# One fused kernel on one Trainium2 core: input sums of the gated layer by transfers instead of elementwise instructions, the expert table's zeros written in the attention stage, and four changes in the order of work

## The chip, the cores and the metric

The kernel runs on one core of one Trainium2 chip. The metric is the device time of one execution, in microseconds; the time of a kernel is the median of its runs.

The core's engines are TensorE (PE in the profile, with PEld its weight loads), VectorE (DVE), ScalarE (ACT), GpSimd (POOL) and SyncE (SP, which here issues transfers). Each works through its own queue of instructions in order. Transfers are issued by SP, ACT or POOL and carried by 16 DMA engines. Tiles live in SBUF, TensorE's results in PSUM banks.

## The reference

Attention over 4 batches, 8 heads, 576 positions and 64 channels, with two kinds of mask; then a gated layer, and then a routed layer with eight experts, of which each token takes one, or none:

```
scores = q @ k.T / 8                  # masked: heads 0-3 see the 32 last positions,
attn   = softmax(scores) @ v          # heads 4-7 every 32nd position before them
x      = attn as (2304 tokens, 512)
x      = (sigmoid(x @ w_gate) * (x @ w_val)) @ w_out         # 512 -> 1536 -> 512
run    = x @ w_skip > 0
e      = argmax(x @ w_gate8)          # over 8 experts, with softmax probability g
out    = x + g * (relu(x @ w1[e]) @ w2[e])   if run, else x  # 512 -> 1024 -> 512
```

## The kernel before

All products of the gated layer and of the experts are made in fp32 precision from two parts: a *high* part (a cast to fp32r on ACT) and a *low* part (the rest, x − high, usually on DVE). A product is three matmuls, high by high, low by high and high by low; the lines L593 to L595 are these three, whatever the product.

**Attention** (to about 131 us) runs in steps t = 0 to 34. What a step does, and in which order it is written, is a string of letters: `eSfEmIFnaNDTMRpDAaL`. `n` and `N` are the scaling of the softmax rows on POOL (`norm`, L314), `f` and `F` the transposes of the result on PE (`flip`, L323), `A` the product with the values (`apply_v`, L339), which copies its result from PSUM on DVE into the tokens' tiles `xf` (L351). `D`, `a` and `p` take one job from the queues of DVE, ACT and POOL. `L` (`step_loads`) fills these queues.

**The gated layer** saves products as Strassen's and Winograd's schemes do: a 2 x 2 block of operands is multiplied with seven products in place of eight. The tokens' operands of a *pair* of token units are the blocks B11, B12, B21 and B22, read from `xf`, and four sums: T1 = B12 − B11, T2 = B22 − T1, T3 = B22 − B12, T4 = B21 − T2 (`combine`, L417). There are three pairs (0, 1, 2) with two units each. `operand` queues the high and the low part of a block or sum. The weights' side has sums too (S1 to S4, `stage_sums`). The **block stage** (about 132 to 397 us) goes over blocks (f, p): weight block f by pair p, 7.28 us each, in the order of the list `BL`; in each, seven products go to the banks A to D of PSUM, and a previous block's results are gated and stored (`store`, L651 to L670) to tables in DRAM, some of them by accumulating transfers that POOL issues (L644). Between the products `background` takes jobs from the three queues by rate, and `need` forces one at once. `split_w` queues the high parts (L534) and low parts (L537) of a weight block: first three quarters of the plain weights, then the four sums. `weights` and `out_weights` queue the conversion of the input weights and of the output weights (`wo`, index arithmetic at L460 and after), in tiles whose places come free as the loads and stores before them end.

**The unit stage** (about 397 to 551 us) makes the output product in 63 steps (`NSTEP`), 21 for each pair; each step is one of the seven products for one of three groups g of channels. It loads tokens' tiles from the tables (`xt`, split at L985 on ACT and L993 on DVE) and weights. Work beside the products hangs on the steps by `at(k, ...)`: the routing of a finished token unit is `turn_back` (three router products on PE at L1086 and L1087, a reduction on DVE at L1089 and a copy on ACT), `pick` (the choice of the expert), and `place` (the rank in the expert's table; then POOL scatters the rows to the table `xs` in DRAM by index). The units of the last pair are u4 and u5. In `init_xs` a tile `zero` is filled by POOL (L1191) and written thirteen times by SP to `xs`, in steps 9 to 15, since the rows that no token takes must be zero and carry a marker.

**The experts** (about 551 to 732 us) read the rows of an expert from `xs`, make the two products (`hidden`, `output_steps`), and scatter the result to the output by index. The first expert's tokens are loaded and cast by `prep` at the end of the unit stage.

Of the kernel before, what the change touches and what calls it, by code (L numbers as in the profile page):

```python
# [23 lines left out]
def kernel(  # L24
# [305 lines left out]
    xf = {}  # L330

    def apply_v(it, s, pT):
# [10 lines left out]
        if ty == 0:  # L343
            for u, o, x, n in spans(b, HS * s, HS * s + HS):
                nc.vector.tensor_copy(xf[u][0][:, hp, o:o + n], pv[:, x - HS * s:x - HS * s + n])
            return
        cl0, ncls = SGRP[s][0], m * n // TPC
        pc = pv.rearrange("p (c t) -> p c t", t=TPC)
        for u, o, x, n in spans(b, 0, S):
            dst = xf[u][1][:, hp, o:o + n].rearrange("p (t c) -> p c t", c=STR)[:, cl0:cl0 + ncls, :]  # L350
            nc.vector.tensor_copy(dst, pc[:, :, x // STR:(x + n) // STR])  # L351
# [58 lines left out]

    def combine(p, nm, eng, parts, cost):

        e = nc.gpsimd if eng == "P" else nc.vector
        for part in parts:
            def fn(part=part):
                x, y = (source(p, z)[:, part, :] for z in SUMS[nm])
                e.tensor_tensor(source(p, nm)[:, part, :], x, y, op=ALU.subtract)  # L417
# [3 lines left out]
    def operand(p, nm, parts, hc, lc):  # L421

        for part in parts:
            def high(part=part):
# [4 lines left out]
                nc.scalar.copy(xh[p, nm][:, part, :], source(p, nm)[:, part, :])  # L429

            def low(part=part):
                h = xh[p, nm][:, part, :]
                nc.vector.tensor_tensor(
                    xl[p, nm][:, part, :], source(p, nm)[:, part, :], h.bitcast(F32), op=ALU.subtract)

            j = Job("A", hc, high, [sum_job[p, nm]] if nm[0] == "T" else [])
            x_jobs.setdefault((p, nm), []).append(Job("D", lc, low, [j]))
# [79 lines left out]
    def stage_sums(f):  # L517
        for i, x, y, op in ((4, 0, 1, ALU.add), (5, 4, 2, ALU.subtract), (6, 2, 0, ALU.subtract), (7, 3, 5, ALU.subtract)):
            def fn(i=i, x=x, y=y, op=op):
                nc.vector.tensor_tensor(stage(f, i), stage(f, x), stage(f, y), op=op)  # L520
# [152 lines left out]
    def period(k, prev):  # L673
# [24 lines left out]
        if prev:  # L698
            prev.mm("D", "A22", "T4", False)
            if prev.p == NP - 1:  # L700
                freed[prev.f].done = clock[0]
            prev.store("sC", "u4", 1)
# [115 lines left out]

    def step_loads(t):
        clock[0] += 1  # L820
        b, j = divmod(t, 8)
# [32 lines left out]
        if t == 22:  # L854
            combine(1, "T1", "P", HALVES, 1.0)
            operand(1, "B11", HALVES, 0.5, 0.5)
        if t == 26:
            for nm in ("T3", "T2", "T4"):
                combine(1, nm, "P", HALVES, 1.0)
            for nm in ("B21", "T3", "T2"):  # L860
                operand(1, nm, HALVES, 0.5, 0.5)
        if t == 30:
            combine(2, "T1", "P", HALVES, 1.0)
# [11 lines left out]
    for t in range(NS + 3):  # L875
        for c in ORDERS.get(t, "eSfEmIFnaNDTMRpDAaL"):
# [17 lines left out]
    raws_left += [(NC - 1, "o")]  # L894
# [12 lines left out]
    for nm in ("T3", "T2", "T4"):  # L907
        combine(2, nm, "D", WHOLE, 0.95)
    for nm in OPS:
# [90 lines left out]
    for f, p in BL:  # L1000
# [5 lines left out]
        if p == 0 and f > 1:  # L1006
            if f + 1 < NC:
                weights(f + 1, more_raw)
            for i in outs_of[f]:
# [63 lines left out]
    def turn_back(u, a):  # L1073
# [7 lines left out]
        for m in range(nb):  # L1081
# [6 lines left out]
            nc.scalar.copy(row[m][:, 256 * a:256 * a + 256].rearrange("p (c n) -> p c n", c=2), pr[:, :, 0:128])  # L1088
            nc.vector.tensor_reduce(  # L1089
                lp[:, m, a, :], pr[:, :, 128:NR].rearrange("p c (t n) -> p n c t", t=2), axis=AX.XY, op=ALU.add  # L1090
            )
            yield
# [94 lines left out]
    zero = []  # L1187

    def init_xs():
        zero = late.tile([128, TW], F32, tag="row", bufs=8, name="zero")  # L1190
        nc.gpsimd.memset(zero, 0.0)  # L1191
        nc.gpsimd.memset(zero[:, TW - 1:TW].bitcast(I32), 1 << 16)
        for i in range(NE * SLOTS // 128):
            nc.sync.dma_start(xs[128 * i:128 * i + 128, :], zero)
            if i % 2:
                yield

# [147 lines left out]
    gx = init_xs()  # L1345
    for k in range(9, 16):
        at(k, gx)
    for p in range(NP):
# [12 lines left out]
        if last:  # L1361
            for k, n in ((15, 1), (16, 2)):
                at(b + k, ta[1], n)
# [3 lines left out]
            for k in range(18, 21):  # L1367
                at(b + k, tb[1])
            g = later(lambda u=ua: place(u, rank_sums(rst[u][1])))
            for k in (19, 20):  # L1370
                at(b + k, g, 3)
# [438 lines left out]
```

## Time and profile before

| what | value |
|---|---|
| median of 3 runs | 747.71 us (747.09 to 747.77) |
| the profiled execution, whole | 746.98 us |
| its span in the trace | 745.3 us, granted TensorE clock 0.99 |
| PE busy | 706.2 us (95%), 4785 matmuls |
| PEld busy | 660.1 us (89%) |
| DVE busy | 561.6 us (75%) |
| ACT busy | 452.0 us (61%) |
| POOL busy | 258.9 us (35%) |
| moved by DMA | 158.57 MB, 213 GB/s in the mean |

The times of the table are of one profiled execution, except the first row. The span is the time from the first to the last instruction that the trace shows; the difference to the whole execution is work around it. A share is busy time over span. A row of a timeline has start, duration, engine, line of the kernel, operation, result and operands with their shapes, the count of equal instructions in a row, and in brackets how long the engine was idle before and which engine and tile ended that.

### The profile page before, as it was taken

The numbers are of one execution on the slowest core, as the hardware profiler recorded it, in microseconds if no ns is written. First come the engines' busy times: TensorE is split into PE (matmuls) and PEld (weight loads), VectorE is DVE, ScalarE is ACT, GpSimd is POOL, SyncE is SP. The second block draws the span as 40 slices with busy tenths as digits, with TensorE's granted clock in tenths as the row PEclk, the third lists the DMA queues.
The fourth block names the chain that finished last, engine by engine and source line by source line (L and its number), as shares of the span: only waits on it lengthen the run. The fifth ranks groups of instructions, "written<-read, shape, count | busy, mean of one in ns | idle before, by whom it ended". The sixth has DMA issues, their size and how long they took to land. (4 is left out here: it accounts for less than half of the span.)

```text
span 745.3 us, 14548 instructions
## 1 busy us (share of the span) xinstructions
PE 706.2 (95%) x4785; PEld 660.1 (89%) x4785; DVE 561.6 (75%) x1246; ACT 452.0 (61%) x1206; POOL 258.9 (35%) x289
## 2 busy tenths in 40 slices
PE   8999988999999999999998989999999999999992
PEld 5766666999999999999888989999988899999991
DVE  3799997989988888888876766677766666666650
ACT  5888986855555555555454855566644766676730
POOL 6577876021040211204033000402324644566611
PEclk9999999999999999999999999999999999999997
DMA  9999610296898888979599996879845687776710
GB/s 199 234 209 220 149 42 30 107 258 187 275 222 256 209 222 228 224 263 202 177 274 335 368 332 180 257 244 303 289 144 186 203 259 246 225 250 223 225 39 14
DMA packets 136857, 158.57 MB, mean 213 GB/s; under 512 B 60510, under 2 KB 105822, under 8 KB 136776
## 3 DMA queue, kind: packets, MB, share of 16 engines
q1 hardware_dynamic: 122072, 134.51, 58.6%
q0 software_dynamic: 11936, 19.66, 12.9%
q10 hardware_dynamic: 2768, 3.41, 1.3%
q8 instruction: 40, 0.66, 0.4%
q14 instruction: 41, 0.34, 0.1%
HBM read 103.49 MB, written 59.65 MB: 219 GB/s over the span
## 5 line engine op out<-in xcount | busy, mean ns | idle before, releaser
L644 POOL DMA_DIRECT2D gT<-sC x36 | 31.9, 1030 | 171.2 <-DVE sC L658 163.9
L301 ACT ACTIVATE sm<-psX,mx 96x128 f32<-96x128 f32 (+2 forms) x176 | 61.8, 375 | 10.1 <-DVE mx L295 7.9
L314 POOL TENSOR_TENSOR sm<-sm,rs 96x384 f32<-96x384 f32 (+2 forms) x64 | 55.5, 885 | 31.6 <-DVE rs L308 18.8
L985 ACT CAST xt<-xt 128x768 fp32r<-128x768 f32 (+1 forms) x74 | 53.9, 742 | 20.5 <-DMA xt<-gB 11.0
L993 DVE TENSOR_TENSOR xt<-xt 128x768 fp32r<-128x768 f32 (+1 forms) x74 | 60.6, 833 | 7.3 <-ACT xt L985 7.2
L639 DVE TENSOR_TENSOR u<-psD,u 128x384 f32<-128x384 f32 x70 | 38.7, 552 | 18.6 <-PE psD L595 18.3
L593 PE MATMUL psD<-xhT,wh 128*128 128x384 f32 x140 | 47.3, 338 | 1.6 <-DVE u L639 1.6
L595 PE MATMUL psA<-xhB,wl 128*128 128x384 f32 x140 | 47.0, 336 | 1.3 <-DVE wl L537 1.3
L595 PE MATMUL psD<-xhT,wl 128*128 128x384 f32 x140 | 47.1, 337 | 0.3 <-DVE wl L537 0.3
L594 PE MATMUL psD<-xlT,wh 128*128 128x384 f32 x140 | 47.0, 336 | 0.0
L594 PE MATMUL psA<-xlB,wh 128*128 128x384 f32 x140 | 46.8, 334 | 0.0
L593 PE MATMUL psA<-xhB,wh 128*128 128x384 f32 x140 | 46.8, 334 | 0.0
L595 PE MATMUL psB<-xhT,wl 128*128 128x384 f32 x140 | 46.8, 334 | 0.0
L593 PE MATMUL psB<-xhT,wh 128*128 128x384 f32 x140 | 46.8, 334 | 0.0
L594 PE MATMUL psB<-xlT,wh 128*128 128x384 f32 x140 | 46.8, 334 | 0.0
L632 ACT COPY psC<-psB 128x384 f32<-128x384 f32 x35 | 16.3, 465 | 43.4 <-PE psB L595 43.4
L1575 POOL DMA_INDIRECT out_dram<-xg x16 | 16.1, 1006 | 73.8 <-DVE xg L1574 65.4
L625 ACT COPY u<-psB 128x384 f32<-128x384 f32 x70 | 33.8, 483 | 11.3 <-PE psB L595 11.1
L1120 POOL COPY row<-lm_all 128x8 f32<-128x8 f32 x18 | 7.9, 478 | 90.1 <-DVE lm_all L1116 90.1
L301 ACT ACTIVATION_READ_ACCUMULATOR sm<-psX,mx 96x1 f32 (+2 forms) x176 | 38.3, 218 | 0.0
L594 PE MATMUL psB<-xt,wtS 128*128 128x384 f32 x108 | 36.3, 336 | 0.9 <-DVE xt L993 0.9
L593 PE MATMUL psB<-xt,wtS 128*128 128x384 f32 x108 | 36.9, 342 | 0.0
(798 smaller groups left out, 2546.7 us busy)
## 6 DMA issues: line engine op xcount, KB each, us to landing
w1r<-in_moe_w_dram SPq DMA_DIRECT2D x28, 512.0 KB
w2r<-in_moe_w_dram SPq DMA_DIRECT2D x28, 512.0 KB
xt<-gT SPq DMA_DIRECT2D x30, 384.0 KB
gT<-u SPq DMA_DIRECT2D x54, 192.0 KB
xt<-gB SPq DMA_DIRECT2D x22, 384.0 KB
gT<-sC POOLq DMA_DIRECT2D x36, 192.0 KB, 6.1
gB<-sA SPq DMA_DIRECT2D x33, 192.0 KB
wg<-in_moe_w_gate_dram SPq DMA_DIRECT2D x12, 512.0 KB
```

Of the source, the lines that this page charges most:

```text
L301: nc.scalar.activation(sm[:n, w, 0:c], src[:, w, :], AF.Exp, bias=mx[:n, w:w + 1], accum_out=sums[:n, h, w:w + 1])
L314: nc.gpsimd.tensor_tensor(x, x, rs[:n, h, 0:m].rearrange("p (w o) -> p w o", o=1).to_broadcast([n, m, c]), op=ALU.mult)
L593: nc.tensor.matmul(ps, lhsT=whi, rhs=xhi, start=start, stop=False, skip_group_check=skip)
L594: nc.tensor.matmul(ps, lhsT=whi, rhs=xlo, start=False, stop=False, skip_group_check=skip)
L595: nc.tensor.matmul(ps, lhsT=wlo, rhs=xhi, start=False, stop=stop, skip_group_check=skip)
L625: nc.scalar.copy(self.tm[nm], self.ps["B"])
L632: nc.scalar.copy(ps, self.ps[src])
L639: nc.vector.tensor_tensor(self.tm[nm], self.ps["D"], self.tm[nm], op=ALU.add)
L644: nc.gpsimd.dma_start(dst, t, accum_op=ALU.add)
L985: nc.scalar.copy(h.bitcast(F32R), l)
L993: nc.vector.tensor_tensor(l.bitcast(F32R), l, h, op=ALU.subtract)
L1575: ins = nc.gpsimd.indirect_dma_start(out=out[:, :], out_offset=bass.IndirectOffsetOnAxis(ap=xg[t][:n, TW - 1:TW].bitcast(I32), axis=0), in ...
```

## The change

Parts that are independent in the code:

- `put_x` writes the blocks B11 and B22 with the opposite sign into `xf`; `operand` turns B11's sign back when it splits it, and the weights' sums change their signs to match. All four sums T become additions.
- For pairs 1 and 2, a sum T is no longer an instruction of POOL or DVE: SP copies one operand into T's tile (`begin_sum`), and POOL then issues a transfer that adds the other operand to it (`combine`). These are spread over steps 23 to 33, and over the end of attention for pair 2. From step 25 the order string has one `p` more at its end. The low parts of B21, T3 and T2 of pair 1 move from DVE to POOL. Pair 2's operands are queued in another order.
- `init_xs` is called at step 29 of attention. Two tiles are filled, and two transfers by SP, which repeat their source, write the whole table.
- When block (0, 2) has ended its last product, the first split of weight block 2 is forced ahead of its store.
- The last raw weights are loaded in another order, and output weight 9 is converted before weight block 11's input weights.
- In the last pair of the unit stage, the routing of u4 and u5 is regrouped on the steps 58 to 62; the reduction of `turn_back` is written ahead of its copy; `prep` moves one step ahead, without the gate (the routing probability) of the rows, which is made later; behind the stage, the choice and the placing of u5 come ahead of the evictions of the first expert's second and third products.

```diff
...
+    def put_x(dst, src, turned):
+        if turned:
+            nc.vector.tensor_scalar(dst, src, -1.0, None, op0=ALU.mult)
+        else:
+            nc.vector.tensor_copy(dst, src)
     def apply_v(it, s, pT):
...
             for u, o, x, n in spans(b, HS * s, HS * s + HS):
-                nc.vector.tensor_copy(xf[u][0][:, hp, o:o + n], pv[:, x - HS * s:x - HS * s + n])
+                put_x(xf[u][0][:, hp, o:o + n], pv[:, x - HS * s:x - HS * s + n], u % 2 == 0)
             return
...
             dst = xf[u][1][:, hp, o:o + n].rearrange("p (t c) -> p c t", c=STR)[:, cl0:cl0 + ncls, :]
-            nc.vector.tensor_copy(dst, pc[:, :, x // STR:(x + n) // STR])
+            put_x(dst, pc[:, :, x // STR:(x + n) // STR], u % 2 == 1)
...
+    def begin_sum(p, nm):
+        nc.sync.dma_start(source(p, nm), source(p, SUMS[nm][0]))
     def combine(p, nm, eng, parts, cost):
-        e = nc.gpsimd if eng == "P" else nc.vector
         for part in parts:
...
                 x, y = (source(p, z)[:, part, :] for z in SUMS[nm])
-                e.tensor_tensor(source(p, nm)[:, part, :], x, y, op=ALU.subtract)
+                t = source(p, nm)[:, part, :]
+                if p == 0:
+                    nc.gpsimd.tensor_tensor(t, x, y, op=ALU.add)
+                else:
+                    nc.gpsimd.dma_start(t, y, accum_op=ALU.add)
             before = [sum_job[p, z] for z in SUMS[nm] if z[0] == "T"]
...
-    def operand(p, nm, parts, hc, lc):
+    def operand(p, nm, parts, hc, lc, eng="D"):
+        turned = nm == "B11"
         for part in parts:
...
                     xl[p, nm] = part_x(f"xl{nm}{p}", l, F32R)
-                nc.scalar.copy(xh[p, nm][:, part, :], source(p, nm)[:, part, :])
+                if turned:
+                    nc.scalar.mul(xh[p, nm][:, part, :], source(p, nm)[:, part, :], -1.0)
+                else:
+                    nc.scalar.copy(xh[p, nm][:, part, :], source(p, nm)[:, part, :])
             def low(part=part):
-                h = xh[p, nm][:, part, :]
-                nc.vector.tensor_tensor(
-                    xl[p, nm][:, part, :], source(p, nm)[:, part, :], h.bitcast(F32), op=ALU.subtract)
+                h, x, l = xh[p, nm][:, part, :].bitcast(F32), source(p, nm)[:, part, :], xl[p, nm][:, part, :]
+                if turned:
+                    nc.vector.scalar_tensor_tensor(l, in0=x, scalar=-1.0, in1=h, op0=ALU.mult, op1=ALU.subtract)
+                else:
+                    (nc.gpsimd if eng == "P" else nc.vector).tensor_tensor(l, x, h, op=ALU.subtract)
             j = Job("A", hc, high, [sum_job[p, nm]] if nm[0] == "T" else [])
-            x_jobs.setdefault((p, nm), []).append(Job("D", lc, low, [j]))
+            x_jobs.setdefault((p, nm), []).append(Job(eng, lc, low, [j]))
...
     def stage_sums(f):
-        for i, x, y, op in ((4, 0, 1, ALU.add), (5, 4, 2, ALU.subtract), (6, 2, 0, ALU.subtract), (7, 3, 5, ALU.subtract)):
-            def fn(i=i, x=x, y=y, op=op):
-                nc.vector.tensor_tensor(stage(f, i), stage(f, x), stage(f, y), op=op)
+        for i, x, y in ((4, 0, 1), (5, 2, 4), (6, 0, 2), (7, 5, 3)):
+            def fn(i=i, x=x, y=y):
+                if i == 7:
+                    nc.vector.scalar_tensor_tensor(
+                        stage(f, i), in0=stage(f, x), scalar=-1.0, in1=stage(f, y), op0=ALU.mult, op1=ALU.subtract)
+                else:
+                    nc.vector.tensor_tensor(
+                        stage(f, i), stage(f, x), stage(f, y), op=ALU.add if i == 4 else ALU.subtract)
             last = Job("D", 0.35, fn)
...
                 freed[prev.f].done = clock[0]
+                if prev.f == 0:
+                    need(w_jobs[2][0])
             prev.store("sC", "u4", 1)
...
+    def init_xs():
+        z, last = temp("zeros"), temp("empty")[:, 0:TW - UT]
+        nc.gpsimd.memset(z, 0.0)
+        nc.gpsimd.memset(last, 0.0)
+        nc.gpsimd.memset(last[:, TW - UT - 1:TW - UT].bitcast(I32), 1 << 16)
+        rows = xs.rearrange("(a p) w -> p a w", p=128)
+        for x, lo, hi in ((z, 0, UT), (last, UT, TW)):
+            nc.sync.dma_start(
+                rows[:, :, lo:hi],
+                x.rearrange("p (o w) -> p o w", o=1).to_broadcast([128, NE * SLOTS // 128, hi - lo]))
     def step_loads(t):
         clock[0] += 1
+        if t == 29:
+            init_xs()
         b, j = divmod(t, 8)
...
                 operand(0, nm, HALVES, 0.5, 0.5)
-        if t == 22:
-            combine(1, "T1", "P", HALVES, 1.0)
+        if t == 23:
+            begin_sum(1, "T1")
             operand(1, "B11", HALVES, 0.5, 0.5)
-        if t == 26:
+        if t == 25:
+            combine(1, "T1", "P", WHOLE, 0.7)
+        if t == 27:
             for nm in ("T3", "T2", "T4"):
-                combine(1, nm, "P", HALVES, 1.0)
-            for nm in ("B21", "T3", "T2"):
-                operand(1, nm, HALVES, 0.5, 0.5)
-        if t == 30:
-            combine(2, "T1", "P", HALVES, 1.0)
+                begin_sum(1, nm)
+            operand(1, "B21", HALVES, 0.5, 0.9, "P")
+        if t == 29:
+            for nm in ("T3", "T2"):
+                combine(1, nm, "P", WHOLE, 0.7)
+        if t == 31:
+            combine(1, "T4", "P", WHOLE, 0.7)
+            begin_sum(2, "T1")
+        if t == 32:
+            for nm in ("T3", "T2"):
+                operand(1, nm, HALVES, 0.5, 0.9, "P")
+        if t == 33:
+            combine(2, "T1", "P", WHOLE, 0.7)
...
     for t in range(NS + 3):
-        for c in ORDERS.get(t, "eSfEmIFnaNDTMRpDAaL"):
+        for c in ORDERS.get(t, "eSfEmIFnaNDTMRpDAaL" + "p" * (t > 24)):
             steps_of[c](t)
...
         raws_left += [(f, "g"), (f, "v")] + [(i, "o") for i in outs_of[f - 1]]
-    raws_left += [(NC - 1, "o")]
+    raws_left[-4:] = [raws_left[i] for i in (-2, -4, -3, -1)] + [(NC - 1, "o")]
...
     for nm in ("T3", "T2", "T4"):
-        combine(2, nm, "D", WHOLE, 0.95)
-    for nm in OPS:
+        source(2, nm)
+    for nm in ("T2", "T3", "T4"):
+        begin_sum(2, nm)
+    for nm in ("T2", "T3", "T4"):
+        combine(2, nm, "P", WHOLE, 0.5)
+    for nm in ("B11", "B21", "B22", "T1", "T3", "T2", "T4"):
         operand(2, nm, WHOLE, 0.8, 0.9)
...
         if p == 0 and f > 1:
+            if f == NC - 2:
+                out_weights(outs_of[f][0], more_raw)
             if f + 1 < NC:
                 weights(f + 1, more_raw)
-            for i in outs_of[f]:
+            for i in outs_of[f][f == NC - 2:]:
                 out_weights(i, more_raw)
...
                 nc.tensor.matmul(pr[:, c, 0:NH], lhsT=sl[:, c, ms], rhs=wri[:, kk, 0:NH], start=False, stop=True)
-            nc.scalar.copy(row[m][:, 256 * a:256 * a + 256].rearrange("p (c n) -> p c n", c=2), pr[:, :, 0:128])
             nc.vector.tensor_reduce(
...
             )
+            nc.scalar.copy(row[m][:, 256 * a:256 * a + 256].rearrange("p (c n) -> p c n", c=2), pr[:, :, 0:128])
             yield
...
     w_e0, pp = [], []
-    zero = []
-    def init_xs():
-        zero = late.tile([128, TW], F32, tag="row", bufs=8, name="zero")
-        nc.gpsimd.memset(zero, 0.0)
-        nc.gpsimd.memset(zero[:, TW - 1:TW].bitcast(I32), 1 << 16)
-        for i in range(NE * SLOTS // 128):
-            nc.sync.dma_start(xs[128 * i:128 * i + 128, :], zero)
-            if i % 2:
-                yield
     PARTS = ((0, HEAD), (HEAD, SLOTS))
...
             at(j + g, do(lambda g=g, nm=nm: w_halves(nm, g)))
-    gx = init_xs()
-    for k in range(9, 16):
-        at(k, gx)
     for p in range(NP):
...
         if last:
-            for k, n in ((15, 1), (16, 2)):
-                at(b + k, ta[1], n)
+            at(b + 16, ta[1], 3)
             g = later(lambda u=ua: pick(u))
...
                 at(b + k, g, 5)
-            for k in range(18, 21):
-                at(b + k, tb[1])
             g = later(lambda u=ua: place(u, rank_sums(rst[u][1])))
-            for k in (19, 20):
-                at(b + k, g, 3)
+            at(b + 19, g, 6)
+            at(b + 20, tb[1], 3)
             break
...
     at(NSTEP - 8, do(fetch_head))
-    at(NSTEP - 2, do(lambda: pp.extend(prep(0, head["xg"], PARTS[:1], tag="Y"))))
+    at(NSTEP - 3, do(lambda: pp.extend(prep(0, head["xg"], PARTS[:1], tag="Y", gates=False))))
...
     hide(0)
-    evict = hidden(1, w, pp, hts, 0, HEAD)
     run(turn_back(NU - 1, 0))
-    evict()
+    evicts = [hidden(1, w, pp, hts, 0, HEAD)]
     run(pick(NU - 1))
-    hide(2, 3)
+    evicts.pop()()
+    evicts = [hidden(f, w, pp, hts, 0, HEAD) for f in (2, 3)]
+    run(place(NU - 1, rank_sums(rst[NU - 1][1])))
+    for evict in evicts:
+        evict()
+    gate(xg, pp, 0, HEAD)
     sums = output_steps(0, HEAD, w, hts, xg, pp, settle)
     run(sums, 2)
-    run(place(NU - 1, rank_sums(rst[NU - 1][1])))
     hide(4)
...
     hide(5)
```

## Rows read from the trace of the kernel before

**Rows 1.** The waits of PE: line waited for what; us in total, times, longest.

```profile
PE psY L323 <- POOL sm L314: 6.2, 18, 0.7
PE psC L593 <- ACT psC L632: 3.6, 1, 3.6
...
PE psD L593 <- DVE u L639: 1.6, 1, 1.6
...
PE psA L595 <- DVE wl L537: 1.3, 1, 1.3
```

**Rows 2.** Windows: PE, PEld, DVE, ACT, POOL busy (count), PEclk, DMA share, GB/s.

```profile
435.00:438.00 3.00, 2.10 (x11) 1.48 (x11) 2.50 (x4) 2.04 (x5) 0.00 (x0) 1.00 1.08 368
116.00:120.00 4.00, 3.57 (x42) 2.66 (x39) 3.90 (x11) 2.93 (x14) 3.17 (x4) 1.00 0.02 4
```

**Rows 3.** Timeline of PE in the unit stage, 437 to 446 us.

```profile
437.43 0.33 PE L1087 MATMUL psY<-wri,sl 128*128 128x138 f32 x1 [0.80 <-DVE sl L1257]
...
443.22 0.34 PE L1086 MATMUL psY<-wri,sh 128*128 128x148 f32 x1 [0.29 <-DVE lp L1089]
...
445.01 0.44 PE L594 MATMUL psB<-xt,wtS 128*128 128x384 f32 x1 [0.90 <-DVE xt L993]
```

**Rows 4.** Timeline of DVE at the end of the block stage.

```profile
365.69 0.43 DVE L460 TENSOR_SCALAR wof<-wo 128x512 int32<-128x512 int32 x1 [2.02 <-DMA wS<-wof]
```

**Rows 5.** Timeline of PE at the end of the unit stage.

```profile
545.05 0.33 PE L1087 MATMUL psY<-wri,s 128*128 128x138 f32 x1 [1.08 <-DVE s L1283]
...
548.67 0.66 PE L1232 MATMUL psY<-ident,xg 128*128 128x128 f32 x4 [0.52 <-DVE base_e L1063]
...
554.82 0.34 PE L1086 MATMUL psY<-wri,s 128*128 128x148 f32 x1 [0.25 <-DVE lp L1089]
```

**Rows 6.** Timeline of ACT, DVE and PE around block 2's split.

```profile
166.29 1.78 ACT L534 CAST wh<-stage 128x768 fp32r<-128x768 f32 x2 [0.38 <-PE psD L594]
...
167.05 0.56 DVE L658 TENSOR_TENSOR sA<-sA,u 128x384 f32<-128x384 f32 x1
...
168.12 2.08 DVE L537 TENSOR_TENSOR wl<-stage,wh 128x768 fp32r<-128x768 f32 x2
...
170.30 0.40 PE L595 MATMUL psD<-xhT,wl 128*128 128x384 f32 x1
```

**Rows 7.** Timeline of POOL in attention, and the fill in the unit stage.

```profile
114.19 0.99 POOL L417 TENSOR_TENSOR xT<-x,xT 128x384 f32<-128x384 f32 x1
115.75 1.53 POOL L314 TENSOR_TENSOR sm<-sm,rs 108x324 f32<-108x324 f32 x2 [0.56 <-DVE rs L308]
...
122.48 1.53 POOL L314 TENSOR_TENSOR sm<-sm,rs 108x324 f32<-108x324 f32 x2 [0.49 <-ACT psX L632]
...
400.68 1.11 POOL L1191 MEMSET zero<- 128x521 f32 x1
```

**Rows 8.** Timeline of PE at attention's end.

```profile
125.91 0.63 PE L323 MATMUL psY<-ident,sm 108*108 108x108 f32 x5
```

**Rows 9.** Issues of L644 (ns min/median/max), POOL's DMA queue from 150 to 175.

```profile
L644 POOL DMA_DIRECT2D gT<-sC x36: 857/895/1379, 152.0 to 398.0; - x36
...
DMA to landing us min/median/max: 3.8/6.2/9.8
...
q0 software_dynamic: 864, 1.18, 28.1%
```

**Rows 10.** Timeline of DVE, ACT and PE, 130 to 149 us.

```profile
130.54 0.77 DVE L351 COPY x<-psY 128x108 f32<-128x108 f32 x2 [1.14 <-PE psY L339]
...
146.41 0.85 ACT L429 CAST xhT<-xT 128x768 fp32r<-128x768 f32 x1
...
148.58 0.33 PE L593 MATMUL psB<-xhT,wh 128*128 128x384 f32 x1
```

**Rows 11.** Timeline of DVE in attention, around 97 us.

```profile
96.70 0.51 DVE L433 TENSOR_TENSOR xlB<-x,xhB 128x384 fp32r<-128x384 f32 x1
...
97.60 1.50 DVE L433 TENSOR_TENSOR xlB<-x,xhB 128x384 fp32r<-128x384 f32 x1
```

## The prediction

> **What bounds the kernel now.** The page comes first: PE is busy 706.2 of 745.3 us at a granted clock of 0.99, so a change moves the time only where it takes away or adds idle time of PE. The waits of PE come second [rows 1]: the largest group is PE behind POOL's softmax scaling in attention (6.2 us in 18 pieces); then single stalls, each ended by one late producer: 3.6 us behind an ACT copy, 1.6 us behind a DVE product, 1.3 us behind a weight's low part. Third, the stages where the edits sit are read instruction by instruction; there the windows tell how full the transfers' engines are. The reader should see that every part of this change meets a different stall, so the sum has six small terms.
>
> **Zeros of the expert table.** Before, thirteen SP transfers of the 128x521 fp32 tile (the last of [rows 7]), 3.47 MB, run in the unit stage. There the transfers move 368 GB/s at a busy share of 1.08 [rows 2], so these are about 9.4 us of all engines' work. PE waits 0.80, 0.29 and 0.90 us there [rows 3], each behind a DVE instruction that splits or reads a token tile just loaded. With 9 us less in front of them these tiles come before they are needed: 0.80 + 0.29 + 0.90 = 1.99 us go. Bounds: 0, if the loads are late for another reason, and 1.99. I take 1.99, since the DMA engines are full there and nowhere else in that stage. The same bytes now go out at step 29 of attention, where the engines' busy share is 0.02 [rows 2]. What hides them is that idleness; without the cover they'd cost up to 9.4 us of delay to the accumulating transfers behind them, which is the slow rival below.
>
> **Order of the last weights.** DVE's index product at 365.69 waits 2.02 us for the transfer that empties its slot [rows 4]; PE then stands 1.64 us behind DVE's product (psD in [rows 1]). Splitting output weight 9 before block 11's weights puts a tile whose slot is free first: −1.64. Bounds −1.64 and 0: the order of the loads doesn't change their sum, so the 3.6 us stall behind ACT (psC in [rows 1]), which comes next, may take it back. I take −1.64, because that stall waits on token tiles and not on these weights.
>
> **Last unit's router.** Two waits of PE, 1.08 and 0.52 us [rows 5], belong to products that wait for a DVE step of the previous product's chain. Moving the three first products one step later and the place step ahead of the last three removes 1.60. Now three products come back to back, twice, with two banks; the third waits for DVE's reduction, for which the nearest row is 0.25 (the last of [rows 5]). I count three such waits: −1.60 + 3 × 0.25 = −0.85. Bounds: −1.60 with none, −0.1 with six.
>
> **Block 2's split.** Before, two highs of 1.78 us together start on ACT at 166.29, and the two lows run on DVE after block (0,2)'s store and gate, 168.12 to 170.20; PE's product with the second low starts at 170.30 [rows 6]. Forcing the first split ahead of the store puts its low in DVE's queue before four elementwise instructions; two of these take the 1.07 from 167.05 to 168.12, so four 2.14 [rows 6]. The first high ends at 166.29 + 0.89 = 167.18; low, four instructions and second low make it 167.18 + 1.04 + 2.14 + 1.04 = 171.40, against 170.30: +1.10. From the other side, PE waits 1.3 us for the first low (psA in [rows 1]), which now is there in time: −1.3 if the second isn't pushed back. I take +1.10: that DVE works in order is what rows 6 show, the lows directly behind the elementwise work.
>
> **Sums by transfers, attention.** Ten POOL subtractions (0.99 for the one in [rows 7]) and three on DVE go. In their place stand eight copies by SP and eight accumulating transfers issued by POOL, and six lows move from DVE to POOL, at about 0.99 each for the same size. In the place of the subtraction at 114.19, ahead of the scaling of 115.75, POOL now gets one low (0.99), fills of the 521 columns that one fill of 1.11 covers before [rows 7], and one issue of an accumulate (0.90, the middle of its kind [rows 9]): 114.19 + 0.99 + 1.11 + 0.90 = 117.19, so the scaling starts 1.4 late. PE waits for these scalings, but has gaps of its own in this stage, so between 0 and +1.4; a little over the middle, +0.8.
>
> Then the accumulates. The sum T4 reads T2, so POOL, which issues T4's accumulate, stands until T2's has landed, and behind it in POOL's queue is the scaling of 122.48 (1.53 us) [rows 7], and behind that PE's flips of 125.91 [rows 8]. T2's accumulate is issued near 118.8, an estimate: the late scaling (117.19 + 1.53) and no more. With x from there to its landing, the flips can start at 118.8 + x + 0.9 for the issue + 1.53 for the scaling = 121.3 + x, rounded up, against 125.91 + 0.8 = 126.7: the loss is max(0, x − 5.4). Before has accumulates from POOL too, 192 KB into the block stage's tables: 3.8 least, 6.2 middle, 9.8 most [rows 9], with the engines busy around them. Here it is 384 KB. POOL's queue moved 1.18 MB in 28.1% of 25 us [rows 9], so 0.168 MB per us of all engines: the further 192 KB take 1.2 us, which makes 5.0 with nothing in the way and 7.4 in a busy time. The zeros (9.4 us from 113 on) are still half in the way: x = 6.2, +0.8. Bounds 0 (x = 5.0) and +4.4 (x = 9.8).
>
> The Trainium skill ("DMA: Bandwidth & Descriptors", Anatomy of one DMA — SWDGE (gpsimd) path) fits such a transfer as 2.0 us plus bytes over 436e3 in us, an estimate of 2.9 us for 384 KB; by it this loss would be 0. The least of the rows, 3.8 for half the bytes, is above that.
>
> **Pair 2.** Its copies start after the last copies out of PSUM at 130.54 [rows 10]; with 0.8 of shift and some 4 us for the rest of the step and a copy (an estimate from the 3.8 of [rows 9]), T2's accumulate is issued near 135.5 and T4's lands at 135.5 + 2x. ACT casts T4 at 146.41 for 0.85, and PE takes the product at 148.58 [rows 10]; that leaves at most 1.3 us, 0.7 as the middle, so with the shift T4 may come at 147.9: the loss is max(0, 2x − 12.4). The zeros are out by then, so x is 5.0: 0; at x = 9.8 it would be 7.2. The three DVE subtractions that go bring nothing: no wait of PE behind DVE there is among its larger ones [rows 1].
>
> The signs, the negated copies and the casts cost what the plain ones did: 0. Sum: −1.99 − 1.64 − 0.85 + 1.10 + 0.80 + 0.80 + 0 = **−1.78 us**. The profiled execution took 746.98, its span 745.3 and 1.7 around it; 746.98 − 1.78 = 745.20. The median of the runs is 0.73 above, so I forecast 747.71 − 1.78 = **745.9**.
>
> **The rivals.**
> *A chain of accumulates (slower).* POOL stands for one landing in attention, and ACT for two in a row for pair 2. From −2.58 (the sum without its last 0.80) the total is −2.58 + (x − 5.4) + (2x − 12.4); it passes +1.5 at x = 7.3. At 8.5 it gives 752.8, at 9.8 756.7. For it: the 3.47 MB of zeros queued in front, and landings up to 9.8 [rows 9]. Against: a busy share of 0.02 before the zeros [rows 2], and zeros done near 125, before pair 2.
>
> *The gains come back (no change).* The 1.64 of the weights' order is paid at the 3.6 us stall [rows 1], and the router's products wait as long as before: 745.9 + 1.64 + 0.85 = 748.4. For it: the loads' sum is unchanged. Against: the stall's own producer is a token tile.
>
> *The split gains (faster).* −1.3 in place of +1.10: 743.5. For it: the 1.3 us wait named psA [rows 1]. Against: DVE's order [rows 6].
>
> *Relief of DVE by a less busy POOL (faster).* The same DVE instruction takes 0.51 us alone and 1.50 us while POOL scales [rows 11]. POOL has ten subtractions fewer and six lows more: four instructions of 0.99 less of such overlap, 3.96 us of DVE's time; if all were on PE's path, 745.9 − 3.96 = 741.9. Against: the lows on POOL slow DVE just as well. The Trainium skill ("GPSIMD Engine Reference", 1. Specifications) says that POOL's ports to SBUF are shared with VectorE when the latter reads two SBUF inputs; the 1.50 agrees, and it speaks against moving the six lows.
>
> **How the numbers follow.** A measurement here tells 0.2%, some 1.5 us, from nothing: faster is below 746.2, slower above 749.2. The forecast's mechanism has 0.55, with a range of its own from 743.5 to 747.5 (the bounds of its terms, not all at once); 0.42 of it lies below 746.2 and 0.13 above. The chain of accumulates has 0.15, all slower; gains coming back 0.12, of which 0.11 is no change and 0.01 slower; the split's gain 0.10 and the relief 0.08, both faster. Faster 0.60, same 0.24, slower 0.16. The range reaches from 741.8, the relief's time, to 749.5, past the gains coming back; it leaves out most of the accumulates' rival (0.13) and some 0.04 below.
>
> **What would show it.** PE's waits behind the three token tiles near 437 to 445 are gone, and so is the 1.64 of psD near 368, with the psC stall still 3.6 or less. The low of block 2's second weight ends later than PE's last product before D. POOL has an idle time in front of its last accumulate of pair 1, ended by a DMA, of x less the time since its issue; its scaling at 122.48 is late by x − 5.4. If ACT waits for a transfer near 147, the slow rival holds. A DVE sum of the elementwise work in 96 to 132 lower by over 3 us, with PE's 6.2 us group smaller, would show the relief. Wrong would be the prediction, above all, if the landing time of an accumulate between tiles isn't near that of one into the tables.

## The result: 1% slower, and the profile after

The changed kernel takes 754.5 us in the median of 5 runs (751.9 to 756.3), against 747.1 in five runs of the kernel before: a ratio of 1.0099, with an interval from 1.0073 to 1.0126. The forecast was 745.9, faster. The span of the profiled execution is 752.8.

The waits of PE after (compare [rows 1]; lines are those of the changed file, L617 is the old L593):

```profile
PE psY L323 <- POOL sm L314: 8.8, 17, 1.5
PE psC L617 <- ACT psC L656: 4.4, 1, 4.4
PE psD L617 <- DVE u L663: 3.1, 1, 3.1
PE psX L617 <- ACT psX L656: 2.6, 2, 2.0
...
PE psD L619 <- DVE wl L561: 1.6, 1, 1.6
```

PE's wait behind POOL has grown by 2.6 us, and the waits behind ACT (psX) and DVE (psD) come from the first blocks. POOL's timeline shows the first (compare [rows 7]):

```profile
114.36 0.89 POOL L430 DMA_DIRECT2D xT<-x  x1 [0.45 <-DVE rs L308]
114.95 1.74 POOL L314 TENSOR_TENSOR sm<-sm,rs 108x324 f32<-108x324 f32 x2
116.31 1.21 POOL L430 DMA_DIRECT2D xT<-xT  x1
118.03 1.17 POOL L314 TENSOR_TENSOR sm<-sm,rs 126x252 f32<-126x252 f32 x2 [0.51 <-DVE rs L308]
126.15 0.88 POOL L430 DMA_DIRECT2D xT<-xT  x1 [6.95 <-DMA xT<-xT]
126.73 1.73 POOL L314 TENSOR_TENSOR sm<-sm,rs 108x324 f32<-108x324 f32 x2
...
135.81 0.89 POOL L430 DMA_DIRECT2D xT<-x  x1 [5.43 <-DMA xT<-x]
...
141.59 0.88 POOL L430 DMA_DIRECT2D xT<-xT  x1 [2.88 <-DMA xT<-x]
143.98 0.86 POOL L430 DMA_DIRECT2D xT<-x  x1 [1.52 <-DMA xT<-x]
147.58 0.85 POOL L430 DMA_DIRECT2D xT<-xT  x1 [2.73 <-DVE xlB L453]
```

Each L430 issues one accumulate. T2's is issued at 116.31, and T4's, which needs it, at 126.15: 9.8 us later, 6.95 of which POOL stands, with a scaling of the softmax behind it. At 135.81 it stands 5.43 us more, now for the *copy* of pair 2's T1, which stands behind the zeros in SP's queue. To issue this copy took SP 9.99 us here, and 0.47 us in `zeros_late`, a run below in which no zeros stand ahead of it:

```profile
116.62 9.99 SPq L419 DMA_DIRECT2D xT<-x  x1
```

```profile
115.47 0.47 SPq L419 DMA_DIRECT2D xT<-x  x1
```

ACT and, behind it, PE stand too. Each cast here waits for T3's accumulate, of pair 1 and then of pair 2; PE's products follow, the second behind DVE, whose low part next to it starts at 151.45, as late as ACT's cast:

```profile
123.09 0.51 ACT L446 CAST xhT<-xT 128x384 fp32r<-128x384 f32 x1 [2.38 <-DMA xT<-x]
...
124.03 0.45 PE L617 MATMUL psX<-xhT,wh 128*128 128x384 f32 x1 [1.98 <-ACT psX L656]
...
151.39 0.84 ACT L446 CAST xhT<-xT 128x768 fp32r<-128x768 f32 x1 [2.90 <-DMA xT<-x]
...
155.13 0.44 PE L617 MATMUL psD<-xhT,wh 128*128 128x384 f32 x1 [3.08 <-DVE u L663]
```

These are the transfers of that time, with size and the median from issue to landing:

```profile
xs<-zeros SPq DMA_DIRECT2D x1, 2496.0 KB, 15.9
xT<-xT POOLq DMA_DIRECT2D x4, 384.0 KB, 8.3
...
xT<-x POOLq DMA_DIRECT2D x3, 384.0 KB, 7.4
xs<-empty SPq DMA_DIRECT2D x1, 890.5 KB, 19.5
```

The zeros take 15.9 and 19.5 us to land, where 9.4 were estimated for both together, and the DMA share from 116 to 132 is 0.99 to 1.20 in every window of 2 us. PE's granted clock falls behind the stalls (windows; columns as in [rows 2]):

```profile
122.00:124.00 2.00, 0.05 (x2) 0.00 (x0) 0.59 (x2) 0.91 (x3) 0.00 (x0) 1.00 1.07 240
...
126.00:128.00 2.00, 0.57 (x5) 0.25 (x4) 0.00 (x0) 0.00 (x0) 1.85 (x3) 1.00 1.15 243
...
130.00:132.00 2.00, 1.39 (x5) 0.89 (x4) 0.23 (x1) 1.10 (x3) 0.38 (x1) 0.50 1.12 245
132.00:134.00 2.00, 2.00 (x10) 1.56 (x10) 0.33 (x1) 1.99 (x4) 0.00 (x0) 0.50 0.62 124
134.00:136.00 2.00, 2.00 (x15) 1.74 (x12) 0.74 (x2) 1.47 (x3) 0.19 (x1) 0.50 0.07 14
```

A granted clock of 0.50 is the lower level, 1.2 GHz. It holds for some 6 us: near 132 us a product of 128x384 starts 0.32 us after the one before it, near 138 us, at 1.00, 0.17 us.

To see where time goes, the table follows one mark through the runs below: the start of ACT's copy of bank B into bank C in a block, in us later than in the kernel before (its marks: 138.0, 168.0, 176.5, 382.3), and the start of the last PE instruction (731.3). Each row is one profiled execution, the last columns all runs.

| kernel | 1st block | 5th | 6th | 34th | last PE | median, us | ratio, interval |
|---|---|---|---|---|---|---|---|
| changed | 5.1 | 9.1 | 11.5 | 9.6 | 8.8 | 754.5 | 1.0099 (1.0073 to 1.0126) |
| zeros_late | −1.6 | 0.2 | 2.6 | 0.7 | 3.0 | 748.3 | 1.0016 (0.9999 to 1.0034) |
| sums_engines | 0.3 | 0.7 | 1.5 | −0.4 | −2.1 | 745.7 | 0.9990 (0.9975 to 1.0005) |
| zeros_late_nosplit | −2.2 | −0.8 | −0.8 | −2.7 | −0.1 | 745.8 | 0.9986 (0.9956 to 1.0017) |
| engines_nosplit | 0.1 | 0.1 | 0.1 | −1.8 | −2.5 | 743.2 | 0.9964 (0.9951 to 0.9977) |
| no_split | 3.7 | 10.3 | 10.3 | 8.4 | 6.4 | 753.7 | 1.0108 (1.0079 to 1.0137) |
| two_orders | 0.6 | 0.6 | 0.6 | −1.3 | −3.3 | 743.6 | 0.9951 (0.9934 to 0.9968) |
| weights_order | 0.0 | 0.0 | 0.0 | −1.8 | −2.7 | 743.8 | 0.9957 (0.9928 to 0.9987) |
| zeros_t24 | 3.4 | 5.6 | 7.9 | 6.0 | 6.2 | 751.2 | 1.0055 (1.0027 to 1.0083) |
| pair1_transfers | −2.0 | −2.0 | −2.0 | −3.9 | 2.7 | 748.1 | 1.0013 (0.9989 to 1.0037) |
| pair1_place | −2.5 | −2.5 | −2.5 | −4.3 | −3.9 | 739.6 | 0.9917 (0.9898 to 0.9937) |
| pair1_place_z33 | −2.2 | −2.2 | −2.2 | −4.1 | −7.7 | 737.8 | 0.9906 (0.9882 to 0.9931) |
| after_place | 3.8 | 10.3 | 12.7 | 10.8 | 9.1 | 756.0 | 1.0127 (1.0107 to 1.0148) |
| transfers_place | −2.0 | 1.8 | 1.8 | −0.1 | −0.4 | 745.4 | 0.9979 (0.9965 to 0.9993) |
| transfers_place_z33 | −1.4 | 12.7 | 12.7 | 10.8 | 9.6 | 754.5 | 1.0106 (1.0085 to 1.0128) |

The medians of the kernel before ran from 745.6 to 747.1 between the groups of runs, so the ratios carry the comparisons.

### The profile page after: what moved, and what is told of

Its sections match the earlier page's. It is cut to its first block, busy times and chain, and to the rows that moved or that the text cites. A ratio compares the mean times of both kernels' runs of the same rounds, so it can differ in the third digit from the quotient of the medians.

```text
span 752.8 us, 14583 instructions
## 1 busy us (share of the span) xinstructions
PE 710.7 (94%) x4785; PEld 664.8 (88%) x4785; DVE 554.1 (74%) x1237; ACT 452.6 (60%) x1206; POOL 259.9 (35%) x294
## 5 line engine op out<-in xcount | busy, mean ns | idle before, releaser
L1047 DVE TENSOR_TENSOR xt<-xt 128x768 fp32r<-128x768 f32 (+1 forms) x74 | 60.8, 835 | 11.5 <-ACT xt L1039 9.8
L314 POOL TENSOR_TENSOR sm<-sm,rs 96x384 f32<-96x384 f32 (+2 forms) x64 | 56.9, 918 | 29.8 <-DVE rs L308 15.9
L1039 ACT CAST xt<-xt 128x768 fp32r<-128x768 f32 (+1 forms) x74 | 54.0, 746 | 19.5 <-DMA xt<-gB 11.5
L617 PE MATMUL psD<-xhT,wh 128*128 128x384 f32 x140 | 47.4, 338 | 3.1 <-DVE u L663 3.1
L617 PE MATMUL psB<-xhT,wh 128*128 128x384 f32 x140 | 47.0, 335 | 0.0
L617 PE MATMUL psA<-xhB,wh 128*128 128x384 f32 x140 | 46.8, 334 | 0.0
L617 PE MATMUL psB<-xt,wtS 128*128 128x384 f32 x108 | 36.9, 342 | 0.0
L323 PE MATMUL psY<-ident,sm 96*128 96x96 f32 (+2 forms) x176 | 27.9, 271 | 9.5 <-POOL sm L314 8.8
L1176 POOL COPY row<-lm_all 128x8 f32<-128x8 f32 x18 | 5.7, 359 | 89.9 <-DVE lm_all L1172 89.9
```

The source lines that it names most:

```text
L314: nc.gpsimd.tensor_tensor(x, x, rs[:n, h, 0:m].rearrange("p (w o) -> p w o", o=1).to_broadcast([n, m, c]), op=ALU.mult)
L323: nc.tensor.transpose(pp[:, w, :], sm[:n, w, 0:c], ident[:n, :n])
L617: nc.tensor.matmul(ps, lhsT=whi, rhs=xhi, start=start, stop=False, skip_group_check=skip)
L1039: nc.scalar.copy(h.bitcast(F32R), l)
L1047: nc.vector.tensor_tensor(l.bitcast(F32R), l, h, op=ALU.subtract)
```

## The experiments

**Zeros or accumulates.** Theory Z: the zeros stand in front of the sums' copies and accumulates. Theory A: accumulating transfers are that slow by themselves. `zeros_late` puts the zeros back:

```diff
...
-        if t == 29:
-            init_xs()
...
+    gx = init_xs()                 # thirteen transfers, as before
+    for k in range(9, 16):
+        at(k, gx)
```

> The changed kernel, with the table's zeros written in the unit stage as before; all else as changed. Theory Z (the zeros' two transfers, 16 and 20 us from issue to landing in the changed kernel, stand in front of the sums' copies and accumulates): the accumulates land in some 5 us in place of 7 to 10, POOL no longer stands 7.0 and 5.4 us for them, the block stage starts at most 1 us later than before in place of 5 to 9, and the time is 748 to 749. Theory A (accumulating transfers are that slow by themselves, whatever else moves): landings stay at 7 us or more, the loss of 5 to 9 us stays, and with the stalls of the unit stage back the time is 754 to 757.

It took 748.3, in Z's range, 6 us under the changed kernel. POOL in that run:

```profile
115.86 1.11 POOL L430 DMA_DIRECT2D xT<-xT  x1
117.48 1.17 POOL L314 TENSOR_TENSOR sm<-sm,rs 126x252 f32<-126x252 f32 x2 [0.51 <-DVE rs L308]
122.11 0.88 POOL L430 DMA_DIRECT2D xT<-xT  x1 [3.46 <-DMA xT<-xT]
...
132.98 0.88 POOL L430 DMA_DIRECT2D xT<-xT  x1 [1.52 <-DMA xT<-x]
```

T2's accumulate is followed by T4's after 6.3 us in place of 9.8, and the first block starts 1.6 us *earlier* than before. One sign of Z did not come: the accumulates that read another sum still took 7.0 us in the median, the others 5.1. `sums_engines` turns it round: zeros at step 29, the sums made by POOL and DVE, in their steps and with their low parts and order as before.

```diff
...
-                if p == 0:
-                    nc.gpsimd.tensor_tensor(t, x, y, op=ALU.add)
-                else:
-                    nc.gpsimd.dma_start(t, y, accum_op=ALU.add)
+                (nc.gpsimd if eng == "P" else nc.vector).tensor_tensor(t, x, y, op=ALU.add)
...
```

> The changed kernel, with all sums made by POOL and DVE as before (their steps, lows and order too); the zeros stay in attention. Theories Z and A agree that attention's loss is gone, since nobody waits for the zeros: what is left is the split (+2.4 and 0.4 after it), the last weights' order (-1.5), 0.3 at the end of the block stage and -2.8 in the unit stage, some 745.9. A rival to both, that the zeros' transfers disturb the loads of weights or the stores of the first blocks by themselves, gives 748 or more, with the first blocks late by 2 us or more.

745.7: neither part alone makes the loss, the two together do. Four kernels without the forced split, all run below, say how much: with neither part the ratio is 0.9951 (`two_orders`), with the sums by transfers alone 0.9986 (`zeros_late_nosplit`), with the early zeros alone 0.9964 (`engines_nosplit`), with both 1.0108 (`no_split`). The two by themselves add 0.48%, some 3.6 us; both together add 1.57%, some 11.7 us, so about 8 us come only where they meet. `zeros_t24` changes one number, `t == 29` to `t == 24`.

> The changed kernel with one number changed: the zeros are written from step 24 of attention, not from step 29. Theory Z (it is where the zeros stand in the queues that matters): they have landed by about 113, the accumulates from 114 on find the engines free, POOL no longer stands 7 and 5.4 us, and the time is 746.5 to 749, as with late zeros. Theory A (accumulates are slow whatever else moves): 752 to 755. A third outcome, that pair 1's copies, which SP issues at step 27 behind the zeros, are now late themselves: 750 to 753, with POOL standing for a copy near 114.

The third outcome, at 751.2. POOL now stands for a copy, which SP issued behind the zeros, with the scaling behind it:

```profile
116.96 0.89 POOL L430 DMA_DIRECT2D xT<-x  x1 [4.22 <-DMA xT<-x]
```

and PE waits 4.59 us for that scaling at 118.67. So for the copies it is the place in SP's queue, not the step, that counts. POOL's accumulates stand in another queue, and what slows those is less plain: the DMA engines were full (0.99 to 1.20), but no run separates that from anything else the zeros do.

**The split.** `no_split` takes out the two lines `if prev.f == 0: need(w_jobs[2][0])`; `zeros_late_nosplit` does so with the zeros late.

> The changed kernel without the forced first split of weight block 2. Theory S (the second low comes too late, PE stands 1.6 us for it and then runs for some 3 us at half its clock): the time falls by 2 to 3 us to about 752, with no stretch at the lower clock near 181. The rival, that the delay between the fifth and the sixth block belongs to the late transfers of pair 2 and comes anyway: no fall, 754 to 755.

> The changed kernel with the zeros in the unit stage as before, and without the forced split; all sums by transfers. The kernel with late zeros and the split took 748.3. Theory S (the split costs its stalls and the half clock behind them, 2.4 there): 745.5 to 746.5, and no stretch at the lower clock near 170 to 175. The rival, that the split costs only what the stalls grow by (2.0 against 1.3 us): 747.3 to 748.

`no_split` at 753.7 lies between the two forecasts and isn't told from the changed kernel by its interval, but its table row loses nothing from the fifth to the sixth block, where the changed kernel loses 2.4. With the zeros late the rows say the same, 2.4 with the split and nothing without; the medians, 745.8 against 748.3, are as theory S had them, though their intervals overlap. In the changed kernel DVE and PE do this (compare [rows 6]; PE's row is the second low's product):

```profile
175.90 0.96 DVE L561 TENSOR_TENSOR wl<-stage,wh 128x768 fp32r<-128x768 f32 x1 [3.58 <-ACT wh L558]
...
178.90 1.22 DVE L561 TENSOR_TENSOR wl<-stage,wh 128x1024 fp32r<-128x1024 f32 x1
```

```profile
180.17 0.45 PE L619 MATMUL psD<-xhT,wl 128*128 128x384 f32 x1 [1.64 <-DVE wl L561]
```

```profile
182.00:184.00 2.00, 2.00 (x8) 2.00 (x7) 1.97 (x5) 0.49 (x1) 0.00 (x0) 0.50 0.00 0
```

Four elementwise instructions stand between the lows, as forecast; the wait of 1.3 us before became 0.36 and 1.64. What was not forecast is the clock of 0.50 behind it. In `sums_engines` the same two waits, 0.36 and 1.64, kept a clock of 1.00 from 168 to 188 us, and the split cost 0.8 us between the marks.

**The orders.** `two_orders` keeps only the sign scheme and the orders of the last weights and of the router; `weights_order` and `router_order` make one of these in the kernel before.

> Only the sign scheme, the order of the last weights and the last unit's router order are left of the change; sums, zeros and split as before. Theory O (the two orders bring what they brought in the changed kernel: 1.5 at the weights, 0.7 in the last pair): 744.5 to 745.5. The rival, that what the weights' order saves is paid at the stall at the end of the block stage: 746.5 to 747.5.

> The kernel before, with the new order of the last weights alone. Theory O (the 1.6 us stall goes and stays gone, nothing else changes): 745.0 to 745.6. The rival W: it also takes away the unit stage's waits of about 2 us, which were not there in the kernel with the two orders although the zeros were written there: 743 to 744. The forecast's third case, that the gain is paid back at the end of the block stage: 746.5 to 747.

> The kernel before with the last unit's router order alone. The forecast's step: the waits of 1.08 and 0.52 us go, some 0.75 comes back, 745.5 to 746.2. The rival (new waits of about 1.2 us behind ACT's copies, as the changed kernel shows them, eat all of it): 746.5 to 747, the same.

`two_orders` gains 0.5% (743.6, below its range), `weights_order` nearly all of it: 743.8, 0.9957 (0.9928 to 0.9987). Its profile shows both the 1.6 us wait gone and, as its rival W said, most of the unit stage's waits gone: of the 1.99 us of [rows 3] one of 0.82 is left. `router_order` is no change: 745.8, 0.9997 (0.9981 to 1.0014); PE's waits of 1.08 and 0.52 us went, and 1.1 us behind ACT's copies came. The same wait in the changed kernel:

```profile
559.63 0.34 PE L1142 MATMUL psY<-wri,s 128*128 128x148 f32 x1 [0.87 <-ACT row L1147]
```

**The zeros' move alone.** `engines_nosplit` is `two_orders` with the zeros at step 29.

> The changed kernel with all sums on POOL and DVE and without the forced split: the two orders, and the zeros in attention at step 29. Against the kernel with the two orders and the zeros in the unit stage (743.6) it tells what the zeros' move alone is worth. The forecast's step (their 9.4 us of transfers out of the unit stage take away 2.0 us of waits): 741.0 to 742.0. The rival (those waits are gone already with the new order of the last weights, so the move is worth nothing): 743 to 744.5.

743.2, 0.9964 (0.9951 to 0.9977), isn't told from `two_orders`. The 2.0 us were not there to be had a second time.

**A better version.** Since sums by transfers made the first block early, and pair 2's chain lost it again, `pair1_transfers` makes only pair 1's sums by transfers (zeros late, no split).

```diff
...
-                if p == 0:
-                    nc.gpsimd.tensor_tensor(t, x, y, op=ALU.add)
+                if p != 1:
+                    (nc.gpsimd if eng == "P" else nc.vector).tensor_tensor(t, x, y, op=ALU.add)
...
```

> Sums of pair 1 by transfers, those of pair 2 by POOL and DVE as before; zeros late, no split, the two orders of the change. Theory R (ten fewer elementwise sums on POOL and DVE relieve attention by about 2 us, as the first block showed it, and what takes it back is pair 2's chain of transfers): the first block 1.5 us earlier than before, nothing lost up to the fifth, 741 to 742.5. The rival, that the transfers give nothing in all: 743 to 744.5, as with sums on the engines (743.6).

Up to the 34th block theory R held, 3.9 us early. But the kernel took 748.1: SP, which issues in order, stood at the end of the block stage, the unit stage's first loads were late, and PE stood 4.70 us for them at 404.67. SP's own wait is the second line:

```profile
379.44 14.76 SPq L1011 DMA_DIRECT2D wtA<-wA  x3
```

```profile
SPq L1011 <- PE psD L619: 13.1, 1, 13.1
```

The kernel with the two orders has 1.91 us there. PE's product into bank D is the one that reads pair 2's T4, the last product of the last block; the reading is that the weight tile wtA12 1 had come to share its bytes with T4's parts. No trace shows the addresses, nor why the place changed; the test is to move it. `pair1_place` does so by one line; `pair1_place_z33` also writes the zeros from step 33, behind pair 1's transfers.

```diff
-    IN_LATE = {(1, nm) for nm in OPS[4:]} | {(2, nm) for nm in OPS[:5]}
+    IN_LATE = {(1, nm) for nm in OPS[4:]} | {(2, nm) for nm in OPS if nm not in ('B11', 'T4')}
```

> Sums of pair 1 by transfers as in the run of 748.1, with one line changed: pair 2's B11 and B22 exchange their areas of SBUF, so that the unit stage's weight tile wtA12 1 no longer shares its bytes with an operand that the last block reads in its last product. Theory P (that shared place held SP's queue 14.8 us, made the first loads of the unit stage late and PE stand 4.7 us): SP stands under 8 us there, the wait of 4.7 is under 1, and the time is 741 to 743. The rival (the loads are late for another reason; early blocks are always paid back at the turn of the stages): 746.5 to 748.5.

> As the kernel with pair 1's sums by transfers and the other place, and the zeros written in attention from step 33, behind pair 1's copies and accumulates. If nobody waits behind them there: first block 1.5 to 2 us early as with late zeros, and 740.5 to 743. If the zeros' 16 us of transfers hold the first blocks' stores or weight loads: the first five blocks lose over 1 us, and the time is 744 or more.

```profile
378.87 2.85 SPq L1011 DMA_DIRECT2D wtA<-wA  x3
```

739.6 and 737.8, both below their ranges: 1% better than the kernel before and 2% better than the changed one. With the zeros behind pair 1's sums, and nobody waiting behind them, they cost nothing; whether they gain the 1.8 us between the two is not settled by the intervals.

**The place in the changed kernel, and zeros between the pairs.** The same line in the changed kernel, and in the kernel with all sums by transfers.

> The changed kernel with the one line of the place (pair 2's B11 and B22 exchange their areas of SBUF). Theory P (in the changed kernel the shared place holds SP 13.2 us at the end of the block stage, and costs what it cost with pair 1's sums: a later start of the unit stage and the lower clock): SP stands under 8 us there, and the time falls by 2 to 4 us, to 750.5 to 752.5. The rival (the other delays cover it): no fall, 754 to 755.

> All sums by transfers, zeros in the unit stage, no forced split (745.8 without it), with the line of the place. Theory P: 742 to 743.5. If the sums of pair 2 by transfers are what keeps this kernel behind the one with pair 1's sums alone (739.6): the difference left, 2 to 3 us, shows in the third block as a wait of 1 us and more of PE behind DVE, which waits for the transfers. The rival, that the place brings nothing here: 745 to 746.5.

> As the kernel before it, with the zeros written in attention from step 33: behind pair 1's sums, but in front of pair 2's copies. Theory Z: pair 2's copies and accumulates stand behind the zeros, so the first four blocks lose 3 us or more against late zeros: 744 to 748. The rival (the zeros are 4 steps later and so out of the way): 741 to 743.

Theory P failed here: 756.0 (1.0127, 1.0107 to 1.0148) and 745.4. SP's stand on wtA fell from 13.2 to 2.2 us in the changed kernel, but the next loads stood in turn, 4.6 us of it for PE's product into bank C:

```profile
398.24 7.95 SPq L1025 DMA_DIRECT2D xt<-gB  x3
```

What holds back the kernel with all sums by transfers is pair 2's chain: 3.8 us between the first and the fifth block, in which PE waits 2.15 and 1.01 us for DVE, and DVE 4.83 us for a transfer. `pair1_place`, with pair 2's sums on the engines, loses nothing there. With the zeros in front of pair 2's transfers, as theory Z had it but for a time far above its range (754.5), this becomes plain; PE stands for DVE, DVE and POOL for transfers:

```profile
PE psD L617 <- DVE u L663: 12.1, 1, 12.1
```

```profile
143.79 0.88 POOL L430 DMA_DIRECT2D xT<-xT  x1 [12.14 <-DMA xT<-x]
...
152.75 0.96 DVE L451 SCALAR_TENSOR_TENSOR xlB<-x,xhB 128x768 fp32r<-128x768 f32 x1 [14.79 <-DMA xT<-x]
```

## Why the prediction was wrong, step by step

**Sums by transfers** is the step that failed, in the size of x and in what it left out. The text took x = 6.2 in attention, with the zeros "half in the way", and 5.0 for pair 2, since "the zeros are out by then". T2 needed 9.8 us from the start of its issue to T4's, and the zeros were on the way until about 133. And the sum looked at accumulates alone: the copies, which SP issues in one queue with the zeros, had no term for being behind them; pair 2's T1 was 9.99 us in the issuing, and POOL stood 5.4 us for it. The experiments show it from both sides: zeros away, −6.2 us (754.5 to 748.3); sums on engines, −8.8 by the medians, −8.1 by the ratios.

The slow rival, a chain of accumulates, named the mechanism and, in attention, the place: POOL stood for T2's landing. At the median of 8.3 us that the changed kernel shows it gives 752.2. For pair 2 it had ACT stand for two accumulates in a row near 147; the trace has POOL stand for a copy first, and ACT 2.90 us for T3's accumulate at 151. It was given 0.15 because a DMA share of 0.02 *before* the change was held against it; but the change itself filled those engines.

The Trainium skill ("DMA: Bandwidth & Descriptors", Anatomy of one DMA — SWDGE (gpsimd) path) gives 2.0 us plus bytes over 436e3, an estimate of 2.9 us for 384 KB. It isn't borne out for these accumulates: even with late zeros the medians were 7.0 and 5.1 us.

**The scaling 1.4 us late** was wrong in sign: the scaling that started at 115.75 before starts at 114.95 in the changed kernel, and with late zeros the first block came 1.6 us early. The changes to pair 1's operands, eight fewer subtractions on POOL and six low parts that go from DVE to POOL, bring some 2 us in attention (pair1_transfers, −2.0); DVE is busy 25.8 us there from 96 to 130, against 29.8 before. This is the rival "relief", with half its price, though that rival held the six low parts to be against it, and no run separates them from the subtractions. Its price was also read loosely: the 0.51 us at 96.70 was not quite alone, since POOL's scaling starts at 96.95.

**The split**, forecast +1.10, cost 0.8 where the clock was kept and 2.4 where it fell, as in the changed kernel: the stalls were sized about rightly, the lower clock behind them was no term of the sum.

**The last weights**, −1.64: right in mechanism; between the sixth and the 34th block the marks gain 1.8 to 1.9 us in each kernel that has it, and the stall behind ACT that was to take this back, 3.6 before, is 3.5 in `two_orders` and 4.4 in the changed kernel. It gained more, 3 us of 747, since most of the unit stage's waits went too. So **the zeros** term of −1.99 was counted a second time: with the weights' order in place the move gave nothing on the engines' kernel. Nor did all three waits stand behind a loaded tile, as the text read them: [rows 3] has only the 0.90 behind the split of one; the 0.80 is behind the low part of a finished result, the 0.29 behind the router's reduction.

**The router's order**, forecast −0.85, gave nothing measurable: the rival "the gains come back" holds for this part alone.

In all, of the forecast's six terms only the weights' came out near its size in the changed kernel, and the two on which the sign hung were sized from rows of a kernel in which the zeros' and the sums' transfers didn't meet.

## What to carry to other kernels

A stretch in which the DMA engines are idle can be filled once: when one change moves two things there, count the second with the first in front of it, queue by queue, copies as well as accumulates. An engine that issues a dependent transfer stood here until the earlier one had landed (POOL 6.95 us), and all that was queued behind it on that engine stood too; give such chains a consumer far away, as pair 1's sums have and pair 2's have not. Terms taken from stalls that follow each other aren't additive: the fix of one may remove the other.

## What the runs showed of the hardware that was not expected

The zeros' two transfers took 9.3 and 14.7 us to land from step 33 (pair1_place_z33), 15.9 and 19.5 beside the sums. The same pair of PE waits, 0.36 and 1.64 us, was followed by a clock near 0.50 in four kernels (changed, zeros_late, zeros_t24, after_place) and by 1.00 in a fifth (sums_engines); what decided it is open. In the kernels with sums by transfers SP's queue stood 11 to 15 us at the end of the block stage, where `two_orders` has 1.9; one line on the places of two operands took this away wherever it was tried, and the time fell with it in one kernel of three.
